# Seven experts in descending token count, with 376 to 448 columns a pass

## Chip, cores and metric

The kernel runs on one core of one Trainium2 chip. The metric is the device time of one execution in microseconds (us), lower is better. TensorE (PE in the profile, PEld for its weight loads) multiplies matrices, VectorE (DVE) and ScalarE (ACT) work on elements, GpSimd (POOL) and SyncE (SP) here mostly issue DMA transfers; the engines run side by side, each through its own list of instructions in order.

## What is computed

Three stages, cut from the reference:

```
for t in range(S):                                   # a linear attention with a complex decay
    S_re, S_im = (ar*S_re - ai*S_im) + k v^T, ar*S_im + ai*S_re
    y[:, :, t] = einsum('bhd,bhde->bhe', q[:, :, t], S_re)
e_idx = argmax(x @ w_gate, axis=1)                   # 3072 tokens, 384 wide, 8 experts
for e in range(8):                                   # one expert per token
    h = maximum(x[mask] @ w1[e], 0)                  # 384 -> 1024
    out[mask] = gate_w * eom * (h @ w2[e])           # 1024 -> 384
h = x @ w_in; g = maximum(0.01*h, h); return g @ w_out   # 384 -> 2048 -> 384
```

Counted from the reference's own gating on its inputs, the experts get 354, 406, 392, 388, 370, 421, 338 and 403 tokens.

## The kernel before, in words

**Attention and routing.** The sequence goes through in six chunks of 128 positions; a planner in Python orders that part. Each chunk's tokens are routed as it ends, and POOL scatters every token's row to a slot of its expert in the DRAM buffer `xs_d`, which has 8 x 448 slots (`CAP` = 448), in the order of the expert's number.

**The experts** (lines 1015 to 1061) follow in the order of their number. Each is two dense layers on 448 columns, whatever its token count. All products are made of three matmuls (`three`, lines 908 to 910) on high and low parts of both operands. The first layer has 8 output blocks `f` of 9 matmuls each (`first_layer`, into the PSUM tile `hp`, 4 buffers); ACT writes the high part `hh` (line 984) and DVE the low part `hl` (line 985). The second layer has 3 output blocks `d` of 24 matmuls (into `yp`); ACT moves each to `yT` and SP stores it (`y_store`, line 977) into `x2_d` at the expert's offset in a compact order, 448 columns wide, so that the next expert overwrites what lies behind the expert's own tokens. That makes 72 + 72 = 144 matmuls an expert. The next expert's slots are loaded into `xe` by SP while the first layer runs (`x_load`, line 889), transposed by PE as 4 x 112 rows (line 903) during the second layer's blocks, and split into `xh` and `xl` (lines 817 and 820).

Expert 0 is special: its first layer runs in two halves of 224 columns (`HALF`), since the first half's slots are complete before the last chunk's tokens have landed.

**Weights.** A list of jobs loads 768 KB pieces on the SP queue into four `raw` buffers, four jobs ahead (`feed`), and each `use()` in the expert loop converts the oldest. A piece of an expert's weights is split into high and low part by ACT and DVE (`wh`, `wl`). A piece of `w_in` or `w_out` is kept as 64-bit numbers and is converted by `d_conv` (one ACT and four DVE instructions, lines 872 to 876), then stored to DRAM (`wf`, line 877) for the last stage. There are 16 of these, d0 to d15. The list before is d0, then for each next expert two pieces of its first layer, a d piece, two of its second layer, a d piece, with d15 extra while expert 2 runs. In the first expert the jobs run after `f` = 0 of the first half, and after `f` = 0, 2 and 4 of the second.

**Places.** After expert 0's first layer `places()` (line 950) sums the counts over the partitions with one matmul, forms the eight offsets `offs` with a chain of eight small additions on DVE, and POOL scatters an (index, weight) pair of every token to `tok_d` (24 indirect DMAs, line 967). From then on SP reads an expert's offset into a register (`values_load`, line 976) before its stores.

**Last stage.** Six windows of 512 columns through `w_in` and `w_out`. In window 5, `flags()` (line 1087) gathers the conditions under which the whole is computed again in a slow general way (an expert with more than 448 tokens is one).

Of the kernel before, what the change touches and what calls it, by code (L numbers as in the profile page):

```python
# [62 lines left out]
def constants():  # L63
    tri = []
    for c in range(2):
        o = token_order(c)
        tri.append((o[:, None] <= o[None, :]).astype(np.float32))
    eye = np.eye(P, dtype=np.float32)
    strict = np.triu(np.ones((P, P), np.float32), 1)
    ones = np.ones((P, P), np.float32)  # L70
    big = np.stack([tri[0], tri[1], 4 * tri[0], 4 * tri[1], eye, strict, ones], 1)
    rev = np.tile(np.arange(NE, 0, -1, dtype=np.float32), B)
    base = np.tile(np.arange(NE, dtype=np.float32) * CAP, B)
    ids = np.arange(P)[:, None] + P * np.arange(NT)[None]
# [283 lines left out]
def tile_kernel(ctx: ExitStack, tc: tile.TileContext, q, k, v, a_re, a_im, wg, w1, w2, w_in, w_out, cbig, csmall, seq, vseq, wgn, out):  # L358
# [22 lines left out]
    IDS = const.tile([P, NT], F32, name="IDS")  # L381
# [5 lines left out]
    offs = const.tile([P, NE + 1], F32, name="offs")  # L387
    offi = const.tile([1, NE], I32, name="offi")
# [401 lines left out]
    raws, wsp, xst, xhl = {}, {}, {}, {}  # L790
    wpool = []

    def w1_src(e, i):
        return w1[e, :, i * 512:(i + 1) * 512].rearrange("(k p) f -> p k f", p=P)

    def w2_src(e, i):
        return w2[e, i * 512:(i + 1) * 512, :].rearrange("(k p) d -> p k d", p=P)

    def pieces(e):
        return [((e, 1, i), w1_src(e, i)) for i in range(2)] + [((e, 2, i), w2_src(e, i)) for i in range(2)]  # L800

    def new_raw(dt=F32):
        return wpool[0].tile([P, 1536], dt, tag="raw", name="raw", bufs=4)

    def w_load(key, src):
        raws[key] = new_raw()
        nc.sync.dma_start(out=raws[key], in_=src)

    nsp = [0]

# [110 lines left out]
    def add_d(n):  # L921
        jobs.append((lambda: d_load(n, d_src(n)), lambda: d_conv(n)))

    add_d(0)
    for e in range(NE - 1):
        for i, p in enumerate(pieces(e + 1)):
            add_w(*p)
            if i % 2:
                add_d(1 + 2 * e + i // 2)
        if e == 2:  # L930
            add_d(15)
    for i in range(4):
        add_w(("in", i), wf[i])
        add_w(("out", i), wf[4 + i])
    done = [0, 0]

    def feed():
        while done[0] < min(len(jobs), done[1] + 4):
            jobs[done[0]][0]()
            done[0] += 1  # L940

# [3 lines left out]
            done[1] += 1  # L945
            feed()

    off = [0] * NE

    def places():  # L950
# [10 lines left out]
        nc.vector.tensor_tensor(out=dl, in0=offs[:, :NE], in1=CS[:, 1, 0], op=ALU.subtract)  # L961
# [3 lines left out]
        nc.vector.tensor_copy(out=pair.bitcast(I32)[:, :, 0], in_=IDS)  # L965
# [48 lines left out]

    for e in range(NE):
        last = e + 1 == NE
        when = {0: 1, 2: 1, 4: 1, 8: 1, 9: 1, 10: 1}
        if e == 2:
            when[5] = 1
        elif last:  # L1020
            when = {0: 1, 1: 1, 2: 1, 3: 1, 9: 1, 10: 1}
        hs = []
        if e == 0:
            hs = [new_h() for f in range(F1 // P)]
            for part in HALF:
                x_split(0, (0, 1, 2), part)
                for f in range(F1 // P):
                    first_layer(0, f, slice(part[0] * SM, part[1] * SM), *hs[f])
                    if part[0]:
                        if f == 0:  # L1030
                            x_load(1)
                        use(when.get(f, 0))
                    elif f == 0:
                        use()
            places()
        else:
            for f in range(F1 // P):
                hs.append(new_h())
                first_layer(e, f, slice(0, CAP), *hs[f])
                if f == 0:  # L1040
                    if last:

# [7 lines left out]
        for d in range(3):  # L1050
            yp = pm.tile([P, 512], F32, name="yp")
            for f in range(F1 // P):
                three(yp[:, :CAP], cols((e, 2, f // 4), (f % 4) * DM + d * P, P), hs[f], f == 0, f == F1 // P - 1)
            yt = ff.tile([P, CAP], F32, name="yT", bufs=4)
            nc.scalar.activation(out=yt, in_=yp[:, :CAP], func=AF.Copy)
            y_store(e, d, yt)
# [27 lines left out]

    bad = const.tile([1, 1], I32, name="bad")

    def flags():

        fl = f2.tile([P, 2], F32, name="fl", bufs=1)
        nc.vector.tensor_reduce(out=fl[:, 0:1], in_=oka, axis=AX.X, op=ALU.min)  # L1090
        nc.vector.tensor_scalar(out=lmin, in0=lmin, scalar1=LMIN2, scalar2=None, op0=ALU.is_ge)
        nc.vector.tensor_reduce(out=fl[0:1, 1:2], in_=lmin, axis=AX.X, op=ALU.min)
        nc.vector.tensor_tensor(out=fl[0:1, 0:1], in0=fl[0:1, 0:1], in1=fl[0:1, 1:2], op=ALU.min)
        cp = pm.tile([P, 512], F32, name="tp")
        for i, (src, n) in enumerate(((acc, NE), (counts[:, 0:1], 1), (fl[:, 0:1], 1))):
            nc.tensor.matmul(out=cp[:, 8 * i:8 * i + n], lhsT=ONES, rhs=src, start=True, stop=True)
        b = f2.tile([1, 3], F32, name="b", bufs=1)
        nc.vector.tensor_reduce(out=b[:, 0:1], in_=cp[0:1, :NE], axis=AX.X, op=ALU.max)
        nc.vector.tensor_scalar(out=b[:, 0:1], in0=b[:, 0:1], scalar1=float(CAP), scalar2=None, op0=ALU.is_gt)
        for i, lim in ((1, CAP / 2), (2, P)):  # L1100
# [58 lines left out]
    slow = nc.values_load(bad[0:1, 0:1], min_val=0, max_val=4)  # L1159
    f2c.close()  # L1160
    pmc.close()
    with tc.If(slow > 0):
# [37 lines left out]
```

## Time and profile before

| | |
|---|---|
| time, median of 3 runs | 935.76 us (935.19 to 937.3) |
| the profiled execution | 935.82 us, span 934.1 us |
| PE, PEld busy | 96%, 84% of the span |
| DVE, ACT, POOL busy | 60%, 50%, 10% |
| granted clock, mean | 0.989 |
| DMA over the span | 121.97 MB, 131 GB/s |

The span is the profiled part of the execution; 1.7 us of its time lie around it. Busy times of PE overlap in part, since matmuls are pipelined and their ends are modelled: how fast matmuls follow each other is read from their starts. An engine with much idle time can still be the one that is waited for in a short stretch.

### The profile page before, as it was taken

Reading aid. Unit: us, or ns where it says so; the run is one execution under the profiler, and the core shown is the slowest. Engines: PE = TensorE matmul, PEld = TensorE weight load, DVE = VectorE, ACT = ScalarE, POOL = GpSimd, SP = SyncE. Lnnn points to the kernel's source line nnn. Section 1 sums busy time; section 2 is a strip of 40 time slices with the busy share of each in tenths; the row PEclk is TensorE's granted clock in tenths of the full one; section 3 lists DMA queues with packets and bytes.
Section 4 is the critical chain, followed back from the end, with each engine's and each line's share of the span. In section 5 each row is a group of like instructions: output and inputs, shape, how many; then the busy total and the mean of one; then the engine's idle time right before and its main releaser. Section 6 shows DMA issues by size and latency. Waiting matters only on the chain.

```text
span 934.1 us, 14772 instructions
## 1 busy us (share of the span) xinstructions
PE 899.2 (96%) x5943; PEld 786.3 (84%) x5943; DVE 564.8 (60%) x964; ACT 469.4 (50%) x765; POOL 96.9 (10%) x90
## 2 busy tenths in 40 slices
PE   7888999999989999999999999999999999999996
PEld 3656878887879899999999899989999998989895
DVE  4679999797877677577566434353363454454332
ACT  6898887877635454444435433333343333333232
POOL 5000302101212810000000000100100100101001
PEclk8999999999999999999999999999999999999999
DMA  9834565212476998777568101302203104000001
GB/s 325 341 91 146 193 239 181 63 53 91 137 249 180 196 239 278 249 252 234 186 216 274 54 1 39 130 1 78 92 1 131 39 0 135 35 1 18 19 1 36
DMA packets 56091, 121.97 MB, mean 131 GB/s; under 512 B 8432, under 2 KB 24480, under 8 KB 56016
## 3 DMA queue, kind: packets, MB, share of 16 engines
q1 hardware_dynamic: 49792, 101.27, 34.7%
q0 software_dynamic: 6224, 19.69, 5.7%
q8 instruction: 48, 0.79, 0.4%
q14 instruction: 27, 0.22, 0.1%
HBM read 89.46 MB, written 31.48 MB: 129 GB/s over the span
## 4 chain that ended last, share of the span: by engine, by line
PE 81%; issue 8%; DVE 5%; ACT 4%; DMA 1%; POOL 1%; SPq 0%; POOLq 0%; another core or an unknown queue 0%; DVEq 0%; ACTq 0%
PE hp L910 10%; PE hp L908 10%; PE hp L909 10%; PE yq L910 6%; PE yq L908 6%; PE yq L909 6%; PE yp L908 4%; PE sc L608 4%; PE yp L909 4%; PE yp L910 4%; PE tp L599 4%; PE yp L620 2%; PE cum L521 2%; PE kv L635 2%; ACT s L453 2%
## 5 line engine op out<-in xcount | busy, mean ns | idle before, releaser
L908 PE MATMUL hp<-xh,wh 128*128 128x512 f32 (+2 forms) x504 | 189.5, 376 | 0.1
L910 PE MATMUL hp<-xh,wl 128*128 128x512 f32 (+2 forms) x504 | 189.4, 376 | 0.0
L909 PE MATMUL hp<-xl,wh 128*128 128x512 f32 (+2 forms) x504 | 188.8, 375 | 0.1
L1139 DVE TENSOR_TENSOR g<-g,hp 128x512 f32<-128x512 f32 x96 | 66.0, 687 | 156.6 <-ACT g L1138 155.0
L1138 ACT ACTIVATE g<-hp 128x512 f32<-128x512 f32 x96 | 57.4, 597 | 186.1 <-PE hp L910 174.9
L908 PE MATMUL yq<-wh,gh 128*128 128x384 f32 x384 | 129.7, 338 | 0.9 <-ACT gh L817 0.9
L910 PE MATMUL yq<-wh,gl 128*128 128x384 f32 x384 | 129.8, 338 | 0.2
L909 PE MATMUL yq<-wl,gh 128*128 128x384 f32 x384 | 129.3, 337 | 0.0
L910 PEld LDWEIGHTS hp<-xh,wl 128*128 128x128 f32 x504 | 95.5, 189 | 15.6
L820 DVE TENSOR_TENSOR gl<-g,gh 128x512 fp32r<-128x512 f32 x96 | 66.5, 692 | 67.1 <-ACT gh L817 45.4
L909 PEld LDWEIGHTS hp<-xl,wh 128*128 128x128 f32 x504 | 95.6, 190 | 11.8 <-DVE xl L820 0.2
L908 PEld LDWEIGHTS hp<-xh,wh 128*128 128x128 f32 x504 | 95.5, 189 | 11.9 <-DVE hl L985 0.5
L817 ACT ACTIVATE gh<-g 128x512 fp32r<-128x512 f32 x96 | 60.7, 632 | 73.6 <-DVE g L1139 73.6
L820 DVE TENSOR_TENSOR wl<-raw,wh 128x1536 fp32r<-128x1536 f32 x40 | 70.2, 1756 | 24.9 <-ACT wh L817 24.1
L1123 POOL DMA_INDIRECT out<-ot,gpair x24 | 24.1, 1005 | 573.4 <-ACT ot L1122 567.4
L908 PEld LDWEIGHTS yq<-wh,gh 128*128 128x128 f32 x384 | 72.1, 188 | 5.9 <-ACT gh L817 1.7
L909 PEld LDWEIGHTS yq<-wl,gh 128*128 128x128 f32 x384 | 72.1, 188 | 4.3
L910 PEld LDWEIGHTS yq<-wh,gl 128*128 128x128 f32 x384 | 72.0, 188 | 0.9 <-DVE gl L820 0.9
L908 PE MATMUL yp<-hh,wh 128*128 128x448 f32 x192 | 71.7, 373 | 0.0
L909 PE MATMUL yp<-hl,wh 128*128 128x448 f32 x192 | 70.3, 366 | 0.0
L910 PE MATMUL yp<-hh,wl 128*128 128x448 f32 x192 | 70.2, 366 | 0.0
L599 PE MATMUL tp<-CB,qk 128*128 128x128 f32 x384 | 56.9, 285 | 9.9 <-DVE qk L555 5.6
(156 smaller groups left out, 1424.4 us busy)
## 6 DMA issues: line engine op xcount, KB each, us to landing
raw<-w SPq DMA_DIRECT2D x32, 768.0 KB
vt<-v SPq DMA_DIRECT2D x12, 512.0 KB
raw<-w_in SPq DMA_DIRECT2D x8, 768.0 KB
wf<-w SPq DMA_DIRECT2D x16, 384.0 KB
raw<-w_out SPq DMA_DIRECT2D x8, 768.0 KB
raw<-wf SPq DMA_DIRECT2D x8, 768.0 KB
xs_d<-zero POOLq DMA_DIRECT2D x4, 1344.0 KB
x_d<-yT SPq DMA_DIRECT2D x24, 224.0 KB
```

Of the source, the lines that this page charges most:

```text
L453: S.op(ACT, 0.04 + A(hi - lo), lambda: nc.scalar.activation(out=out.ap(lo, hi), in_=in_.ap(lo, hi), **kw), in_.b(lo, hi), out.b(lo, hi), p ...
L521: S.op(PE, 0.64, lambda fp=fp, a=a, z=z: nc.tensor.matmul(out=fp.t, lhsT=TRI[c % 2], rhs=th.ap(a, z), start=True, stop=True), [cbb] + th.b ...
L599: nc.tensor.transpose(tp.t[:, h, :], src.t[:, h0 + h].rearrange("p a d -> p (a d)"), IDN)
L608: nc.tensor.matmul(out=sc.t[:, h, :], lhsT=kT.t[:, h], rhs=qT.t[:, h], start=True, stop=True)
L817: nc.scalar.activation(out=hi, in_=src, func=AF.Copy)
L820: nc.vector.tensor_tensor(out=lo, in0=src, in1=hi, op=ALU.subtract)
L908: nc.tensor.matmul(out=out, lhsT=ah, rhs=bh, start=first, stop=False)
L909: nc.tensor.matmul(out=out, lhsT=ah, rhs=bl, start=False, stop=False)
L910: nc.tensor.matmul(out=out, lhsT=al, rhs=bh, start=False, stop=last)
L1123: put = nc.gpsimd.indirect_dma_start(out=rows, out_offset=bass.IndirectOffsetOnAxis(ap=gpair.bitcast(I32)[:, j, 0:1], axis=0), in_=ot, in_ ...
L1138: nc.scalar.activation(out=g, in_=hp, func=AF.Copy, scale=0.01)
L1139: nc.vector.tensor_tensor(out=g, in0=g, in1=hp, op=ALU.max)
```

## The change

The seven experts after expert 0 run in descending order of their token count, and the expert at place n runs with `CAPS[n]` columns. A slot load still takes 448 rows in 112 partitions, and PE still transposes all of them. What is narrower is the split of the transposed slots, every matmul and evacuation of the two layers, and the stores. Expert 0 stays first, with 448. For this the order must be known before the first weights of place 1 are loaded: a new `ranks()` after `f` = 4 of expert 0's first half compares the counts and writes, by place, the expert, its slot base and its offset to `plani`, from which SP reads registers. Until then the list of jobs may issue three loads only, so three d pieces now come first, and the weights of place 1 after them; d3 follows these, and from expert 2 on each expert has two. `flags` is called in two steps, at `f` = 2 and 6, and compares each place's count with its own bound.

```diff
+CAPS = (448, 448, 432, 424, 408, 400, 384, 376)
...
+    def reg(n, r):
+        if (n, r) not in regs:
+            top = (NE - 1, (NE - 1) * CAP, NTOK)[n]
+            regs[n, r] = nc.values_load(plani[0:1, n, r:r + 1], engines=[mybir.EngineType.SP], min_val=0, max_val=top)
+        return regs[n, r]
+
+    def one(w, r):
+        return w[bass.ds(reg(0, r), 1)].rearrange("o a b -> (o a) b") if r else w[0]
...
-        return nc.sync.dma_start(out=xst[e][:, a:z], in_=xs_d[e * CAP + a * SM:e * CAP + z * SM].rearrange("(s p) d -> p s d", p=SM))
+        src = xs_d[bass.ds(reg(1, e), CAP)] if e else xs_d[a * SM:z * SM]
+        return nc.sync.dma_start(out=xst[e][:, a:z], in_=src.rearrange("(s p) d -> p s d", p=SM))
...
-        cs = slice(part[0] * SM, part[1] * SM)
+        cs = slice(part[0] * SM, min(part[1] * SM, CAPS[e]))
...
-    add_d(0)
-    for e in range(NE - 1):
-        for i, p in enumerate(pieces(e + 1)):
+    for n in range(3):
+        add_d(n)
+    for p in pieces(1):
+        add_w(*p)
+    add_d(3)
+    for e in range(2, NE):
+        for i, p in enumerate(pieces(e)):
             add_w(*p)
             if i % 2:
-                add_d(1 + 2 * e + i // 2)
-        if e == 2:
-            add_d(15)
+                add_d(2 * e + i // 2)
...
-        while done[0] < min(len(jobs), done[1] + 4):
+        while done[0] < min(len(jobs), done[1] + 4, limit[0]):
...
+    def ranks():
         cp = pm.tile([P, 512], F32, name="tp")
         nc.tensor.matmul(out=cp[:, :NE], lhsT=ONES, rhs=acc, start=True, stop=True)
-        nc.vector.memset(offs[:, 0:1], 0.0)
-        for e in range(NE):
-            nc.vector.tensor_tensor(out=offs[:, e + 1:e + 2], in0=offs[:, e:e + 1], in1=cp[:, e:e + 1], op=ALU.add)
-        nc.vector.tensor_copy(out=offi, in_=offs[0:1, :NE])
+        vec.tensor_copy(out=num, in_=cp[:, :NE])
...
+        vec.tensor_tensor(out=more, in0=inner(key), in1=outer(key), op=ALU.is_gt)
+        vec.tensor_reduce(out=rank, in_=more, axis=AX.X, op=ALU.add)
...
+        for n, src in ((1, base), (2, offs), (3, num)):
+            vec.tensor_tensor(out=more, in0=sel, in1=inner(src), op=ALU.mult)
+            vec.tensor_reduce(out=plan[:, n], in_=more, axis=AX.X, op=ALU.add)
...
+        vec.tensor_copy(out=plani, in_=plan[0:1, :3])
+        limit[0] = len(jobs)
...
-        if e and d == 0:
-            off[e] = nc.values_load(offi[0:1, e:e + 1], engines=[mybir.EngineType.SP], min_val=0, max_val=NTOK)
-        nc.sync.dma_start(out=x2_d[d][:, bass.ds(off[e], CAP)] if e else x2_d[d][:, :CAP], in_=yt)
+        nc.sync.dma_start(out=x2_d[d][:, bass.ds(reg(2, e), CAPS[e])] if e else x2_d[d][:, :CAPS[0]], in_=yt)
...
-        if e == 2:
-            when[5] = 1
+        if e == 0:
+            when = {0: 1, 3: 1, 5: 1, 8: 1, 9: 1, 10: 1}
...
-                    elif f == 0:
+                    elif f in (0, 2):
                         use()
+                    elif f == 4:
+                        ranks()
+                        feed()
...
-            if i == 5 and f == 4:
-                flags()
+            if i == 5 and f in (2, 6):
+                flags(f > 2)
```

The change moves instructions on two engines in expert 0's first half. On DVE (`w` is the converted d piece, `hl` the low part of a block of the first layer, `xl` that of the slots), before:

```order
L985 SCALAR_TENSOR_TENSOR hl<-hp,hh 128x224
L873 TENSOR_SCALAR w_3524<-raw 128x768
...
L876 SCALAR_TENSOR_TENSOR w_3524<-expo,w_3524 128x768
L985 SCALAR_TENSOR_TENSOR hl<-hp,hh 128x224 x7
L820 TENSOR_TENSOR xl<-tp,xh 128x224 x3
L985 SCALAR_TENSOR_TENSOR hl<-hp,hh 128x224
```

And now:

```order
L1021 SCALAR_TENSOR_TENSOR hl<-hp,hh 128x224 x2
L889 TENSOR_SCALAR w_3555<-raw 128x768
...
L892 SCALAR_TENSOR_TENSOR w_3555<-expo,w_3555 128x768
L1021 SCALAR_TENSOR_TENSOR hl<-hp,hh 128x224 x2
L978 COPY num<-tp 128x8
...
L991 CAST plani<-plan 1x24
L1021 SCALAR_TENSOR_TENSOR hl<-hp,hh 128x224 x3
L836 TENSOR_TENSOR xl<-tp,xh 128x224 x3
```

A second conversion and the 17 small instructions of `ranks` now stand ahead of the three `xl` that the second half's matmuls read.

On SP, from the first loads of the expert stage on, before (`xe` are the slots, `wf` the stores of converted pieces):

```order
L889 DMA xe<-xs_d 112x2x384
L863 DMA raw<-w_in 128x3x512
L807 DMA raw<-w 128x3x512 x2
L863 DMA raw<-w_in 128x3x512
L889 DMA xe<-xs_d 112x2x384
L877 DMA wf<-w_3524 128x768
L807 DMA raw<-w 128x4x384
L889 DMA xe<-xs_d 112x4x384
L807 DMA raw<-w 128x4x384
```

And now:

```order
L879 DMA raw<-w_in 128x3x512 x3
L906 DMA xe<-xs_d 112x2x384
L893 DMA wf<-w_3523 128x768
L893 DMA wf<-w_3555 128x768
L803 TENSOR_LOAD plani
L803 ISA x2
L823 ISA
L823 DMA raw<-w 128x3x512
...
L823 DMA raw<-w 128x4x384
L803 TENSOR_LOAD plani
...
L906 DMA xe<-xs_d 112x4x384
L893 DMA wf<-w_3702 128x768
L823 ISA
L823 DMA raw<-w 128x4x384
```

The weights of place 1 moved from ahead of the second slot load to behind the two `wf` stores and the read of `plani`.

## Rows read from the trace of the kernel before

**Rows 1.** Windows by stage: expert 0's first layer; the other seven experts

```profile
core 0: us, PE busy (x) PEld busy (x) DVE busy (x) ACT busy (x) POOL busy (x), PEclk, DMA share, GB/s
268.40:289.10 20.70, 19.74 (x154) 18.90 (x155) 13.58 (x26) 10.72 (x23) 1.04 (x2) 0.92 0.55 168
...
305.30:519.70 214.40, 213.14 (x1080) 195.34 (x1079) 140.90 (x161) 101.10 (x141) 22.00 (x18) 1.00 0.78 230
```

**Rows 2.** Timeline of SP: start, us, ...: first store of experts 0, 1, 2, 7

```profile
294.88 0.37 SPq L977 DMA_DIRECT2D x_d<-yT  x1
...
325.50 0.38 SPq L977 DMA_DIRECT2D x_d<-yT  x1
...
357.57 0.37 SPq L977 DMA_DIRECT2D x_d<-yT  x1
...
510.69 10.14 SPq L977 DMA_DIRECT2D x_d<-yT  x3
```

**Rows 3.** Timeline of PE: matmuls 8 apart (224, 448 columns), 11 apart (384)

```profile
277.58 0.28 PE L908 MATMUL hp<-xh,wh 128*128 128x224 f32 x1
...
278.47 0.28 PE L910 MATMUL hp<-xh,wl 128*128 128x224 f32 x1
...
292.27 0.36 PE L908 MATMUL yp<-hh,wh 128*128 128x448 f32 x1
...
293.90 0.37 PE L910 MATMUL yp<-hh,wl 128*128 128x448 f32 x1
...
542.20 0.34 PE L908 MATMUL yq<-wh,gh 128*128 128x384 f32 x1
...
544.15 0.34 PE L910 MATMUL yq<-wh,gl 128*128 128x384 f32 x1
```

**Rows 4.** Timeline of DVE: expert 0's first half, then `places`

```profile
271.51 0.55 DVE L873 TENSOR_SCALAR w<-raw 128x768 int32<-128x768 int32 x1
...
275.03 1.28 DVE L985 SCALAR_TENSOR_TENSOR hl<-hp,hh 128x224 fp32r<-128x224 f32 x4
277.16 0.39 DVE L985 SCALAR_TENSOR_TENSOR hl<-hp,hh 128x224 fp32r<-128x224 f32 x1 [0.85 <-ACT hh L984]
278.17 0.39 DVE L985 SCALAR_TENSOR_TENSOR hl<-hp,hh 128x224 fp32r<-128x224 f32 x1 [0.62 <-ACT hh L984]
279.18 0.39 DVE L985 SCALAR_TENSOR_TENSOR hl<-hp,hh 128x224 fp32r<-128x224 f32 x1 [0.61 <-ACT hh L984]
279.48 0.68 DVE L820 TENSOR_TENSOR xl<-tp,xh 128x224 fp32r<-128x224 f32 x2
...
292.65 1.49 DVE L956 TENSOR_TENSOR offs<-offs,tp 128x1 f32<-128x1 f32 x8
...
294.31 0.36 DVE L962 TENSOR_TENSOR hd<-hot,dl 128x192 f32<-128x192 f32 x1
```

**Rows 5.** Windows around the start of expert 0's matmuls

```profile
265.45:268.86 3.41, 1.82 (x13) 1.43 (x14) 2.64 (x20) 1.35 (x6) 2.50 (x4) 1.00 0.92 346
268.86:272.28 3.42, 3.42 (x18) 3.42 (x17) 1.43 (x4) 1.40 (x3) 0.89 (x1) 0.50 0.33 121
```

**Rows 6.** Line 976: the read of an offset into a register of SP

```profile
L976 SPq TENSOR_LOAD <-offi x7: 268/482/810, 320.1 to 503.2; - x7
```

**Rows 7.** Timelines of SP and ACT: a load of a weight piece, and its first reader

```profile
493.29 0.44 SPq L807 DMA_DIRECT2D raw<-wf  x1
...
499.34 1.49 ACT L817 ACTIVATE wh<-raw 128x1536 fp32r<-128x1536 f32 x1 [0.95 <-DMA raw<-wf]
```

**Rows 8.** Timelines of SP and PE: expert 2's slot load, and its first transposes

```profile
308.60 1.09 SPq L889 DMA_DIRECT2D xe<-xs_d  x1
...
326.16 0.96 PE L903 MATMUL tp<-CB,xe 112*128 112x112 f32 x8 [1.26 <-issue]
```

**Rows 9.** Windows: during POOL's scatter of places, and three experts later

```profile
300.00:345.00 45.00, 43.74 (x223) 39.91 (x222) 29.29 (x34) 22.51 (x31) 26.35 (x21) 1.00 0.99 201
390.00:480.00 90.00, 90.00 (x462) 82.58 (x460) 59.26 (x67) 40.78 (x59) 0.00 (x0) 1.00 0.71 228
```

**Rows 10.** Waits of the last stage: who waited for whom, us, times, longest

```profile
PE tp L1096 <- DVE fl L1093: 0.9, 1, 0.9
```

More of the change, by code (lines that the diff above doesn't have):

```diff
@@ L791, in tile_kernel, with w1_src, w2_src, pieces @@
     wpool = []
[L793 to L800, printed above, removed]
+    regs = {}
+    def reg(n, r):
[5 more added lines that the diff above has]
+        return w[bass.ds(reg(0, r), 1)].rearrange("o a b -> (o a) b") if r else w[0]
+    def w1_src(r, i):
+        return one(w1, r)[:, i * 512:(i + 1) * 512].rearrange("(k p) f -> p k f", p=P)
+    def w2_src(r, i):
+        return one(w2, r)[i * 512:(i + 1) * 512, :].rearrange("(k p) d -> p k d", p=P)
+    def pieces(r):
+        return [((r, 1, i), lambda i=i: w1_src(r, i)) for i in range(2)] + [((r, 2, i), lambda i=i: w2_src(r, i)) for i in range(2)]
     def new_raw(dt=F32):
@@ L806, in w_load @@
         raws[key] = new_raw()
-        nc.sync.dma_start(out=raws[key], in_=src)
+        nc.sync.dma_start(out=raws[key], in_=src())
     nsp = [0]
@@ L946, in use, with places @@
             feed()
-    off = [0] * NE
-    def places():
+    def ranks():
         cp = pm.tile([P, 512], F32, name="tp")
         nc.tensor.matmul(out=cp[:, :NE], lhsT=ONES, rhs=acc, start=True, stop=True)
-        nc.vector.memset(offs[:, 0:1], 0.0)
-        for e in range(NE):
-            nc.vector.tensor_tensor(out=offs[:, e + 1:e + 2], in0=offs[:, e:e + 1], in1=cp[:, e:e + 1], op=ALU.add)
-        nc.vector.tensor_copy(out=offi, in_=offs[0:1, :NE])
+        num, key, rank = (ff.tile([P, NE], F32, name=nm, bufs=1) for nm in ("num", "key", "rank"))
+        more, sel = (ff.tile([P, NE, NE], F32, name=nm, bufs=1) for nm in ("more", "sel"))
+        base = CS[:, 1, 0]
+        inner = lambda t: t.unsqueeze(1).to_broadcast([P, NE, NE])
+        outer = lambda t: t.unsqueeze(2).to_broadcast([P, NE, NE])
+        vec = nc.vector
+        vec.tensor_copy(out=num, in_=cp[:, :NE])
+        vec.scalar_tensor_tensor(out=key, in0=base, scalar=-1.0 / (16 * CAP), in1=num, op0=ALU.mult, op1=ALU.add)
+        vec.tensor_scalar(out=key[:, 0:1], in0=key[:, 0:1], scalar1=1.0e4, scalar2=None, op0=ALU.add)
+        vec.tensor_tensor(out=more, in0=inner(key), in1=outer(key), op=ALU.is_gt)
+        vec.tensor_reduce(out=rank, in_=more, axis=AX.X, op=ALU.add)
+        vec.tensor_scalar(out=rank, in0=rank, scalar1=float(CAP), scalar2=None, op0=ALU.mult)
+        vec.tensor_tensor(out=sel, in0=inner(rank), in1=outer(base), op=ALU.is_equal)
+        vec.tensor_tensor(out=more, in0=more, in1=inner(num), op=ALU.mult)
+        vec.tensor_reduce(out=offs, in_=more, axis=AX.X, op=ALU.add)
+        for n, src in ((1, base), (2, offs), (3, num)):
+            vec.tensor_tensor(out=more, in0=sel, in1=inner(src), op=ALU.mult)
+            vec.tensor_reduce(out=plan[:, n], in_=more, axis=AX.X, op=ALU.add)
+        vec.tensor_scalar(out=plan[:, 0], in0=plan[:, 1], scalar1=1.0 / CAP, scalar2=0.25, op0=ALU.mult, op1=ALU.add)
+        vec.tensor_copy(out=plani, in_=plan[0:1, :3])
+        limit[0] = len(jobs)
+    def places():
         dl = ff.tile([P, NE], F32, name="dl", bufs=1)
@@ L960, in places @@
         sh = ff.tile([P, NT], F32, name="sh", bufs=1)
-        nc.vector.tensor_tensor(out=dl, in0=offs[:, :NE], in1=CS[:, 1, 0], op=ALU.subtract)
+        nc.vector.tensor_tensor(out=dl, in0=offs, in1=CS[:, 1, 0], op=ALU.subtract)
         nc.vector.tensor_tensor(out=hd, in0=hot, in1=dl.unsqueeze(1).to_broadcast([P, NT, NE]), op=ALU.mult)
@@ L964, in places @@
         nc.vector.tensor_tensor(out=cpos, in0=sh, in1=slot, op=ALU.add)
-        nc.vector.tensor_copy(out=pair.bitcast(I32)[:, :, 0], in_=IDS)
+        nc.vector.tensor_copy(out=pair.bitcast(I32)[:, :, 0], in_=IDS[:, :NT])
         for j in range(NT):
@@ L1038, in tile_kernel @@
                 hs.append(new_h())
-                first_layer(e, f, slice(0, CAP), *hs[f])
+                first_layer(e, f, slice(0, cap), *hs[f])
                 if f == 0:
@@ L1052, in tile_kernel @@
             for f in range(F1 // P):
-                three(yp[:, :CAP], cols((e, 2, f // 4), (f % 4) * DM + d * P, P), hs[f], f == 0, f == F1 // P - 1)
+                three(yp[:, :cap], cols((e, 2, f // 4), (f % 4) * DM + d * P, P), [h[:, :cap] for h in hs[f]], f == 0, f == F1 // P - 1)
             yt = ff.tile([P, CAP], F32, name="yT", bufs=4)
-            nc.scalar.activation(out=yt, in_=yp[:, :CAP], func=AF.Copy)
-            y_store(e, d, yt)
+            nc.scalar.activation(out=yt[:, :cap], in_=yp[:, :cap], func=AF.Copy)
+            y_store(e, d, yt[:, :cap])
             if d < 2:
@@ L1085, in tile_kernel, with flags @@
     bad = const.tile([1, 1], I32, name="bad")
[L1087 to L1093, printed above, removed]
-        cp = pm.tile([P, 512], F32, name="tp")
[L1095 to L1100, printed above, removed]
+    fl = f2.tile([P, 2], F32, name="fl", bufs=1)
+    b = f2.tile([1, NE + 2], F32, name="b", bufs=1)
+    def flags(step):
+        if step == 0:
+            nc.vector.tensor_reduce(out=fl[:, 0:1], in_=oka, axis=AX.X, op=ALU.min)
+            nc.vector.tensor_scalar(out=lmin, in0=lmin, scalar1=LMIN2, scalar2=None, op0=ALU.is_ge)
+            nc.vector.tensor_reduce(out=fl[0:1, 1:2], in_=lmin, axis=AX.X, op=ALU.min)
+            nc.vector.tensor_tensor(out=fl[0:1, 0:1], in0=fl[0:1, 0:1], in1=fl[0:1, 1:2], op=ALU.min)
+            nc.vector.tensor_tensor(out=b[:, 2:], in0=plan[0:1, 3], in1=IDS[0:1, NT:], op=ALU.is_gt)
+            return
+        cp = pm.tile([P, 512], F32, name="tp")
+        for i, src in enumerate((counts[:, 0:1], fl[:, 0:1])):
+            nc.tensor.matmul(out=cp[:, 8 * i:8 * i + 1], lhsT=ONES, rhs=src, start=True, stop=True)
+        for i, lim in ((0, CAP / 2), (1, P)):
             nc.vector.tensor_scalar(out=b[:, i:i + 1], in0=cp[0:1, 8 * i:8 * i + 1], scalar1=float(lim), scalar2=None, op0=ALU.is_lt)
@@ L1158, in tile_kernel @@
     assert done[1] == len(jobs)
-    slow = nc.values_load(bad[0:1, 0:1], min_val=0, max_val=4)
+    slow = nc.values_load(bad[0:1, 0:1], min_val=0, max_val=NE + 2)
     f2c.close()
```

17 lines of the change are left out of this document (10 added, 7 removed).

## The prediction

> **What bounds the kernel now.** I read the windows by stage first, then the starts of the stores, then PE's own starts. In the stretch of the seven experts after expert 0 PE is busy 213.1 of 214.4 us at granted clock 1.00, DVE 140.9 and ACT 101.1 [rows 1]: PE bounds it, and nothing else is near. The stores show the same as a beat: between the first stores of experts 0 and 1 lie 30.62 us, between those of experts 1 and 2 32.07, and from expert 2 to expert 7 five times (510.69 - 357.57) / 5 = 30.62 [rows 2]. The one long beat holds a wait of 1.26 us before the transposes of expert 2's slots [rows 8]. A busy PE is not yet a PE whose time goes with the columns. So I take the starts: 8 matmuls of 224 columns take 278.47 - 277.58 = 0.89 us, 111 ns each; 8 of 448 take 293.90 - 292.27 = 1.63 us, 204 ns; 11 of 384 take 1.95 us, 177 ns [rows 3]. From 224 to 448 that is (204 - 111) / 224 = 0.413 ns a column, and from 384 to 448 (203.8 - 177.3) / 64 = 0.414: a straight line with some 19 ns beside the columns. With it 144 x 0.204 = 29.3 us of a beat are such matmuls; the rest are transposes, which the change leaves.
>
> Expert 0's first layer is another matter. There DVE works 13.6 of 20.7 us [rows 1], but in bursts: the conversion of a d piece holds it from 271.51 to 275.03, 3.5 us, and behind it the blocks' low parts queue; after that it waits for ACT 0.85, 0.62 and 0.61 us and goes on at 279.48 with the `xl` on which PE's second half waits [rows 4]. The idle time in the first half that can take up more DVE work is therefore about 2.1 us.
>
> **The change part by part.**
>
> *Narrower passes.* By place they cut 0, 0, 16, 24, 40, 48, 64 and 72 columns, 264 in all. Times 144 matmuls times 0.413 ns that is 15.7 us, all on PE's path, since PE is the bound there [rows 1, 3]: **-15.7**. ACT, DVE and the stores get shorter too, which is worth nothing by itself. DVE's load stays under PE's: even unshortened its 140.9 us are 71% of what is left, 214.4 - 15.7. Slot loads and transposes stay whole. The row stands against a rule here. The Trainium skill (TensorE: Matmul & The Clock Gate, Back-to-back issue gap) says that in streams of weight load and matmul the spacing is set by both, with about 81 ns at 128 columns and 131 at 512. By these two figures a column would be worth 0.13 ns and the cut 5 us, an estimate from that page; the three spacings measured here lie on a line three times as steep.
>
> *Expert 0's first half on DVE.* New ahead of the second half's `xl` are one conversion, 3.5 us [rows 4], and `ranks`: 17 dependent instructions, 11 of which touch 64 elements a partition and 6 eight or fewer. The nearest rows are the chain of eight single additions, 1.49 / 8 = 0.19 us each, and the 192-element product, 0.36 [rows 4]. All at the first, they cost 3.2 us; the 11 at the second, 5.1; I take 0.25 for the 11, since 64 lies a third of the way, and have 3.9. Together 7.4, less the idle 2.1: the second half starts 5.3 us later. PE stands still meanwhile, first because the buffers of `hp` are full (block 7 needs the low part of block 3, behind the second conversion), then for `xl`. After such a pause the clock can fall: in 3.4 us in which PE was busy 1.8 the clock was 1.00, and in the 3.4 after it 0.50, the lower level of 1.2 GHz [rows 5]. A second fall would cost half of 3.4, 1.7 us; since the conversion of d2 then holds `hp` anyway, I count 0.7. **+6.0** in all. As bounds I take 3.5, if the cheap instructions also fill gaps that I don't see and the clock stays, and 3.5 + 5.1 - 2.1 + 1.7, about 8.5.
>
> *Weights of place 1.* Their loads move behind the two `wf` stores and the register read (0.27 to 0.81 us [rows 6]). The order is ready on DVE at about 275.0 + 0.6 (two low parts) + 3.5 + 0.6 + 3.9 = 283.6; the first piece is issued near 285. A piece needed 6.05 us from issue to reader [rows 7], so near 291 it is there. Its split stands behind block 3 of the second half, which ends near 285.4 + 4.0 + 1.5 (late `xl`, slow clock) = 291. It just fits; if it is late by a microsecond, ACT holds blocks 4 to 7 back, whose high and low parts are needed only in the second layer, from 295 on. **0**, at most +2. The slots of place 1 are issued behind three pieces, near 287, for transposes near 300, 13 us later.
>
> *Later loads.* From expert 1 on the jobs come in the same rhythm as before, without d15 in expert 2, whose third conversion cost PE nothing (its beat was 30.62 too [rows 2]). The registers cost SP under 1 us apiece [rows 6] beside waits that are longer. The wait for the slots of the third expert [rows 8] stays, as it did not come from the columns: **0**, from -1.3 to +3.
>
> *Flags.* PE waited 0.9 us in the last stage for DVE's chain in `flags` [rows 10]. With the chain four blocks ahead of the matmuls that wait is gone: **-0.9**. The shorter `places` saves DVE 1.5 us where PE doesn't wait for it: 0.
>
> Sum: -15.7 + 6.0 - 0.9 = -10.6. Against the profiled execution, 935.82 us (934.1 span and 1.7 around it), that gives 925.2; the median of the runs is 0.06 lower. I forecast **925 us**.
>
> **The rivals.**
>
> *The first expert pays almost nothing.* The added DVE work would have to find more gaps than the 2.1 us, and a loss of 1.5 us would give 935.8 - 16.6 + 1.5 = 920.7. For it speaks that PE's own second half takes 9 us while DVE's share in it is unchanged; against it, that `xl` stands behind all of the new work on an in-order engine. Chance 0.10.
>
> *Loads behind the ranking come late.* Expert 2's slots were 326.16 - 308.60 = 17.6 us on their way [rows 8], while the transfer share was 0.99 and only 201 GB/s moved [rows 9]. If place 1's slots took as long from 287, PE would wait from 300 to 304.6: 4.6 us more, 929.8; with the second place's slots also 3 us worse, 933. Against it: at 287 POOL's scatter has not begun. Chance 0.20.
>
> *The weight loads set a floor.* PEld is busy 195.3 us for 1079 loads, 0.181 us each [rows 1]. If matmuls could not follow each other faster than that, the cut would end at (204 - 181) / 0.413 = 56 columns: places 6 and 7 would give 56 instead of 64 and 72, 240 in all, 14.3 us, and the time would be 926.6. By the Trainium skill's rule above, which goes further, there would be no gain (935.8 - 5 - 0.9 + 6). The spacing of 111 ns at 224 columns, under loads of the same size, speaks against both. Chance 0.03.
>
> *Transfers become the bound, and it is slower.* A beat moves 228 GB/s x 30.62 us = 7.0 MB for an expert [rows 9, 2]; narrower passes ask for it in 26 to 30 us. In the scatter stretch 201 GB/s was all there was at share 0.99. At that rate through all seven experts each would take 34.7 us, 243 in place of 214.4, and the kernel would take 935.8 + 5.1 + 28.6 = 969 us. It is slower than before from the point where the seven take over 214.4 - 5.1 = 209.3 us, that is under 233 GB/s. Against it: three experts later 228 GB/s took a share of 0.71 only [rows 9], so some 320 are to be had once the scatter is over. The Trainium skill (DMA: Bandwidth & Descriptors, Queues, rings and completion order) has each DMA engine take turns between the queues it has work for; the fall to 201 GB/s while POOL scatters agrees. Chance 0.05.
>
> *The change doesn't do what it says.* Were a place's count over its columns, the whole would be computed again in the general way. The seven counts, descending, are 421, 406, 403, 392, 388, 370 and 338, each under its columns by at least 12. Chance 0.01.
>
> **How the numbers follow.** The forecast has the remaining 0.61, with a range of its own from 922.5 to 928. The low end of the whole takes every bound at its best, 935.8 - 15.7 - 0.9 - 1.3 + 3.5 = 921.4, and a part of the first rival; the high end takes 935.8 - 16.6 + 8.5 + 3 = 930.7, and the first price of the late loads: 920.5 to 931. Left out are the rest of the late loads (0.08), transfers (0.05), the fall-back (0.01) and the tail of the first rival (0.04), under 0.2. Within 0.2% is about what a measurement here can tell from no change, 933.9 to 937.6. Faster by more: the forecast, the first three rivals but for 0.02, 0.92. Within: those 0.02 and 0.02 of mild transfer trouble, 0.04. Slower: the other 0.03 of transfers and the fall-back, 0.04.
>
> **What would show it.** A beat between first stores holds 48 matmuls of one place and 96 of the next, so the beats that end at places 3 to 7 should be 30.62 less 0.413 ns for each of their cut columns: 29.4, 28.6, 27.9, 27.1 and 26.5; the one that ends at place 2 30.0 and the wait for slots, 31.3. DVE should work without a gap from the first conversion to the second half's `xl`, which should stand near 284.8 instead of 279.48, with the clock at 0.50 somewhere behind; expert 0's first store should stand near 301. The wait at the flags should be missing. Wrong would be: beats that don't fall with the columns (a floor, or transfers); waits of ACT for `raw` or of PE before the transposes in places 1 and 2 (late loads); no gap on PE in the first half (the first rival).

## Result and the profile after

The changed kernel takes 924.53 us (median of 4 runs, 921.46 to 926.62) beside 936.39 for the kernel before on the same chip (935.19 to 937.3): ratio 0.9872, interval 0.9841 to 0.9902. It is faster, by 11.9 us, and the forecast of 925 is met. The profiled execution took 924.78 us with a span of 923.0, which compares with 935.82 and 934.1.

The windows by stage of the kernel after (columns as in [rows 1]), and four at half clock, three at the start of expert 0's matmuls and one behind its pause:

```profile
268.40:289.10 20.70, 15.13 (x97) 14.24 (x97) 15.37 (x48) 6.44 (x17) 1.95 (x2) 0.75 0.29 93
...
305.30:519.70 214.40, 211.85 (x1165) 205.19 (x1164) 144.03 (x167) 105.01 (x152) 26.00 (x22) 1.00 0.82 232
...
265.45:268.86 3.41, 2.37 (x12) 2.00 (x12) 1.52 (x12) 0.98 (x4) 2.40 (x3) 0.50 0.42 158
268.86:272.28 3.42, 2.79 (x14) 2.30 (x14) 2.05 (x12) 1.07 (x3) 1.49 (x2) 0.50 0.25 92
272.28:275.69 3.41, 3.41 (x20) 3.41 (x20) 2.16 (x4) 1.52 (x3) 0.00 (x0) 0.56 0.50 149
...
285.50:292.30 6.80, 5.33 (x25) 5.33 (x26) 4.35 (x12) 1.89 (x4) 0.00 (x0) 0.50 0.64 211
```

Against [rows 1], PE gets less done in the window that held expert 0's first layer, 15.1 us busy where there were 19.7, and DVE more, 15.4 for 13.6; the clock's mean fell from 0.92 to 0.75. In the stretch that held the seven other experts PE is nearly as full as before, and more work passes in the same 214.4 us: 1165 matmul records in place of 1080.

The first stores of the eight places after (SP's timeline), which answer to [rows 2]:

```profile
303.39 0.37 SPq L1013 DMA_DIRECT2D x_d<-yT  x1
...
333.86 0.38 SPq L1013 DMA_DIRECT2D x_d<-yT  x1
...
365.01 0.36 SPq L1013 DMA_DIRECT2D x_d<-yT  x1
...
393.74 0.37 SPq L1013 DMA_DIRECT2D x_d<-yT  x1
...
421.66 0.36 SPq L1013 DMA_DIRECT2D x_d<-yT  x1
...
449.17 0.36 SPq L1013 DMA_DIRECT2D x_d<-yT  x1
...
476.06 0.34 SPq L1013 DMA_DIRECT2D x_d<-yT  x1
...
502.04 8.57 SPq L1013 DMA_DIRECT2D x_d<-yT  x3
```

The beats are 30.47, 31.15, 28.73, 27.92, 27.51, 26.89 and 25.98 us, 198.65 in all, where the kernel before has 510.69 - 294.88 = 215.81.

DVE's timeline after, expert 0's first half (columns as in [rows 4]; `dest` is the last slot that the stage before works out, `num` and `plani` the first and last step of `ranks`):

```profile
269.90 0.16 DVE L706 SCALAR_TENSOR_TENSOR dest<-rs,slot 128x1 int32<-128x1 f32 x1
...
273.77 0.55 DVE L889 TENSOR_SCALAR w<-raw 128x768 int32<-128x768 int32 x1
...
277.29 0.68 DVE L1021 SCALAR_TENSOR_TENSOR hl<-hp,hh 128x224 fp32r<-128x224 f32 x2
277.89 0.55 DVE L889 TENSOR_SCALAR w<-raw 128x768 int32<-128x768 int32 x1
...
281.40 0.68 DVE L1021 SCALAR_TENSOR_TENSOR hl<-hp,hh 128x224 fp32r<-128x224 f32 x2
282.00 0.16 DVE L978 COPY num<-tp 128x8 f32<-128x8 f32 x1
...
285.56 0.17 DVE L991 CAST plani<-plan 1x24 int32<-1x24 f32 x1
285.65 0.97 DVE L1021 SCALAR_TENSOR_TENSOR hl<-hp,hh 128x224 fp32r<-128x224 f32 x3
286.55 0.67 DVE L836 TENSOR_TENSOR xl<-tp,xh 128x224 fp32r<-128x224 f32 x2
```

The waits of ACT that stood in [rows 4] are gone, DVE goes from the first conversion (273.77) through the second and `ranks` (282.00 to 285.65, 3.65 us) to the second half's `xl` without a gap, and PE waits for it. PE's waits after (who waited for whom: us in total, times, longest):

```profile
PE tp L920 <- DVE xl L836: 4.1, 2, 3.5
...
PE tp L920 <- DMA xe<-xs_d: 1.6, 1, 1.6
PE hp L925 <- DVE hl L1021: 1.5, 1, 1.5
```

In the kernel before the same `dest` ends the stage ahead:

```profile
267.76 0.16 DVE L702 SCALAR_TENSOR_TENSOR dest<-rs,slot 128x1 int32<-128x1 f32 x1
```

With it the span splits into four pieces:

| piece | before, us | after, us | difference |
|---|---|---|---|
| start to the last `dest` | 267.76 | 269.90 | +2.1 |
| last `dest` to expert 0's first store | 27.12 | 33.49 | +6.4 |
| the seven beats | 215.81 | 198.65 | -17.2 |
| last place's first store to the end | 423.4 | 421.0 | -2.4 |
| span | 934.1 | 923.0 | -11.1 |

### The profile page after: what moved, and what is told of

It is laid out like the page before. It is cut to its first block, busy times and chain, and to the rows that moved or that the text cites. A ratio compares the mean times of both kernels' runs of the same rounds, so it can differ in the third digit from the quotient of the medians.

```text
span 923.0 us, 14884 instructions
## 1 busy us (share of the span) xinstructions
PE 884.9 (96%) x5941; PEld 786.1 (85%) x5941; DVE 562.1 (61%) x970; ACT 466.1 (50%) x765; POOL 96.2 (10%) x90
## 4 chain that ended last, share of the span: by engine, by line
PE 79%; issue 8%; DVE 7%; ACT 3%; DMA 2%; POOL 1%; SPq 0%; POOLq 0%; another core or an unknown queue 0%; DVEq 0%; ACTq 0%
PE hp L927 10%; PE hp L926 10%; PE hp L925 9%; PE yq L927 6%; PE yq L925 6%; PE yq L926 6%; PE sc L612 4%; PE tp L603 4%; PE yp L925 4%; PE yp L926 4%; PE yp L927 4%; PE yp L624 2%; PE cum L525 2%; PE kv L639 2%; PE yp L628 1%
## 5 line engine op out<-in xcount | busy, mean ns | idle before, releaser
L925 PE MATMUL hp<-xh,wh 128*128 128x512 f32 (+8 forms) x504 | 187.0, 371 | 1.5 <-DVE hl L1021 1.5
L927 PE MATMUL hp<-xh,wl 128*128 128x512 f32 (+8 forms) x504 | 187.5, 372 | 0.0
L926 PE MATMUL hp<-xl,wh 128*128 128x512 f32 (+8 forms) x504 | 187.5, 372 | 0.0
L925 PE MATMUL yp<-hh,wh 128*128 128x448 f32 (+6 forms) x192 | 68.3, 356 | 0.0
L926 PE MATMUL yp<-hl,wh 128*128 128x448 f32 (+6 forms) x192 | 67.1, 349 | 0.0
L927 PE MATMUL yp<-hh,wl 128*128 128x448 f32 (+6 forms) x192 | 67.1, 349 | 0.0
```

Of the source, the lines that this page charges most:

```text
L925: nc.tensor.matmul(out=out, lhsT=ah, rhs=bh, start=first, stop=False)
L926: nc.tensor.matmul(out=out, lhsT=ah, rhs=bl, start=False, stop=False)
L927: nc.tensor.matmul(out=out, lhsT=al, rhs=bh, start=False, stop=last)
```

## Experiments

They ran in three groups, each on a chip of its own with runs of the kernel before beside it; ratios are to those. Where a size of a few us matters I compare the pieces of the table, in each run's own trace, since the piece ahead of the last `dest` varies (below).

**fixed: the columns alone.** The kernel before, cut by expert number:

```diff
+CAPS = (448, 432, 408, 400, 384, 448, 376, 424)
...
-                first_layer(e, f, slice(0, CAP), *hs[f])
+                first_layer(e, f, slice(0, CAPS[e]), *hs[f])
...
-                    three(yp[:, :CAP], ...
+                    three(yp[:, :CAPS[e]], ...
```

> The kernel before with the same 264 columns cut, by expert number (widths fitted to the counts of these inputs), and without any ranking, moved load or change at the flags. Theory: 935.8 less 15.7, so 920 us, with 918 if the faster spacing that the change's trace shows beside the narrower columns (3.4 us over seven beats) belongs to the narrowing itself; expert 0's first store stays within 1 us of 295 unless the clock falls earlier. Rival (a floor under the spacing): 921.5 or above.

Measured: 920.18 us beside 935.53, ratio 0.9834 (0.9821 to 0.9847), 15.35 us less for 264 columns; the rival's 921.5 was not reached, and neither was the 918 that faster spacing through narrowing would have given. First and last of its first stores:

```profile
294.53 0.37 SPq L978 DMA_DIRECT2D x_d<-yT  x1
...
495.49 0.35 SPq L978 DMA_DIRECT2D x_d<-yT  x1
```

Its way from the last `dest` (267.30) to the first store is 27.23, as before, so nothing but the beats (200.96 in place of 215.81) and the last expert's rest moved. The columns pay by themselves, at 15.35 / (264 x 144) = 0.404 ns each in a matmul.

**p448: all but the narrowing.**

```diff
-CAPS = (448, 448, 432, 424, 408, 400, 384, 376)
+CAPS = (448,) * 8
```

> The change with 448 columns at every place: experts still go by count and are ranked in expert 0's first half, only the narrowing is undone. Theory (columns pay 0.413 ns each per matmul, the ranking costs 6): the seven beats between the stores of d0 go back to about 30.6 us, and the time is the change's 924.5 plus 15.7 to 18.5, so 940 to 943, 4 to 7 above the kernel before. Rival 1 (part of the gain comes from the shifted addresses of the tiles or another side effect of the change, not from the columns): beats near 29.8 and the time 935 to 937. Rival 2 (a column is worth 0.13 ns): 924.5 plus 5, 930.

Measured: 936.42 beside 935.53, ratio 1.0017 (1.0003 to 1.003). The order without the narrowing gains nothing, but it was expected to lose 4 to 7, and rival 1 has the number. Its way to the first store is 299.87 - 266.79 = 33.08, so the ranking costs 6.0 there as in the change; the beats gave it back: 211.43 us, most of them 30.02 or 30.14 where the kernel before has 30.62. PE's timeline shows why, six starts apart:

```profile
428.57 0.36 PE L927 MATMUL yp<-hh,wl 128*128 128x448 f32 x1
...
429.77 0.36 PE L927 MATMUL yp<-hh,wl 128*128 128x448 f32 x1
```

1.20 / 6 = 0.200 us for one of 448 columns, where [rows 3] give 0.204. Counted as one cycle of 2.4 GHz a column (0.417 ns, near the 0.413 of the prediction's line; 448 / 2.4 = 187) that is 13 ns beside the columns in place of 17. Between p448 and the change lie 1.0017 - 0.9872 = 1.45%, 13.6 us, but the intervals leave some 10 to 17, which does not set it apart from 15.4. By the pieces of the two traces the narrowing is worth 211.43 - 198.65 = 12.8 in the beats and 1.0 behind them.

**pad, pad64, pad128, before_again: is it where the tiles lie?** The change's new constants move xh, hh and what follows by 192 bytes. The kernel before with a spare tile, of 48, 16 or 32 floats:

```diff
+    spare = const.tile([P, 48], F32, name="spare")
+    nc.gpsimd.memset(spare, 0.0)
```

> The kernel before with one more constant tile of 192 bytes a partition, so that the tiles behind it lie 192 bytes further on, as in the change; nothing else. Rival (the faster spacing in the change, about 13 ns beside the columns where there were about 18, comes from where the tiles lie): 448-column matmuls of the seven beats at 0.200 us, beats near 30.1, time 931 to 932. Theory (addresses have no part in it): beats of 30.6 and 935 to 937.

> The kernel before with a spare constant tile of 64 bytes a partition; nothing else. Asks what of the address decides the spacing beside the columns (17.8 ns on average in the kernel before, 13.3 in the 192-byte shift from the fourth expert on). If it is the offset within 128 bytes (64 shifts it as 192 does): beats from the fourth expert on of 30.0 to 30.15. If any shift does it: the same here and with 128 bytes. If it is not the address but how PE's stream happens to fall in a run: either value, or a change from one to the other within the run.

> The kernel before with a spare constant tile of 128 bytes a partition; nothing else. Offset within 128 bytes decides: as before, beats of 30.62. Any shift decides: 30.0 to 30.15. Neither, but the run: either value, or a change within the run.

> The kernel before once more, unchanged. If the spacing of its 448-column matmuls belongs to the addresses, the beats are 30.62 again, on whatever chip; if to the run, 30.0 or a change within the run can come out. From the last dest to the first store: 27.1 again.

The last three ran once each. Measured: with 192 bytes ratio 1.0004 (0.9994 to 1.0013), 936.48 us; so in time the rival misses. But the spacing did move. PE's timeline in one run of it (938.5 us), expert 1 and then expert 3:

```profile
335.28 0.37 PE L910 MATMUL yp<-hh,wh 128*128 128x448 f32 x1
...
335.90 0.37 PE L910 MATMUL yp<-hh,wh 128*128 128x448 f32 x1
...
385.27 0.36 PE L910 MATMUL yp<-hh,wh 128*128 128x448 f32 x1
...
385.87 0.36 PE L910 MATMUL yp<-hh,wh 128*128 128x448 f32 x1
```

Three starts take 0.62 us in the first and 0.60 in the second: 0.207 and 0.200 in one run, the same widths and the same lines. Beats are 30.01 to 30.14 but for the one with the slot wait (34.60), and what they give is taken by that wait and by the last stage, which is 2.7 us longer (936.7 - 510.56 = 426.1). With 64 bytes the first beat is 30.15 and the last five are 30.62; with 128 all seven are 30.73 to 30.75. The kernel before gives 30.62 again on another chip (31.25 in the second beat, which has 32.07 in the first run). So the offset within 128 bytes is not it, and shifts do not all act alike; the value mostly repeats with the layout, and can change within a run. What sets it stays open.

One part of before_again's expectation missed: from the last `dest` to the first store it took 293.80 - 265.86 = 27.94, not 27.1 again.

```profile
265.86 0.16 DVE L702 SCALAR_TENSOR_TENSOR dest<-rs,slot 128x1 int32<-128x1 f32 x1
...
293.80 0.37 SPq L977 DMA_DIRECT2D x_d<-yT  x1
```

Its half clock ahead of expert 0 lasted some 6.8 us, where the first run of the kernel before had 3.4. With fixed and the three spare tiles, this way takes 26.75 to 27.94 us without `ranks`.

**after64: the change at the old offsets.** The same spare tile of 16 floats in the change, which makes the shift 256 bytes.

> The change with a spare constant tile of 64 bytes, which puts the blocks' tiles at the offsets within 256 bytes that they have in the kernel before. If the addresses gave part of the gain: the seven beats sum to 201 to 202 in place of 197.5 to 198.7, as in the kernel with fixed widths, and the time is 3 to 4 longer than the change's (ratio 0.990 for 0.987). If they have no part: the change's beats and ratio.

Measured: ratio 0.988 (0.9863 to 0.9898), beats 198.81 us in all. A miss: 201 to 202 were expected. Its five narrow beats (29.19, 28.17, 27.68, 26.62, 26.17) are together 0.8 longer than the change's. But it had no wait for slots, where the change had 1.6: it is 1.8 longer than the change without that wait, and 1.35 longer than after_again (below), which had none either. Of the change's gain, then, some 1.4 to 1.8 us may belong to the layout, not 4.

**after_again: the change once more.**

> The changed kernel once more, unchanged. If the spacing belongs to the addresses and widths, the seven beats come out as in its first profile within 0.1 us each (30.5, 31.1, 28.7, 27.9, 27.5, 26.9, 26.0); if it belongs to the run, some differ by 0.5. If the long half clock ahead of expert 0 (10 us in the first profile, 3.4 in the kernel before) belongs to the run, it differs here, and expert 0's first store stands between 300 and 303.4; from the last dest to that store it stays 33.0 to 33.5.

Measured: ratio 0.9864 (0.9832 to 0.9897). The five narrow beats come out as before to 0.01 us; the two 448-wide ones at the start do not (30.92 and 29.51 for 30.47 and 31.15, the second without a wait for slots). The last `dest` stands at 265.28 in place of 269.90, with half clock for some 3.4 us ahead of expert 0 instead of 10; the way to the first store is 298.23 - 265.28 = 32.95, and that store stands earlier than the 300 to 303.4 expected. So the +2.1 of the table belongs to the run, the narrow beats and the longer way to the change.

**early: no conversion in expert 0's first half, the ranking at once.**

```diff
-    for n in range(3):
-        add_d(n)
+    add_d(0)
...
-    add_d(3)
+    add_d(1)
...
-    done, limit = [0, 0], [3]
+    done, limit = [0, 0], [1]
...
-                    elif f in (0, 2):
-                        use()
-                    elif f == 4:
+                    elif f == 0:
                         ranks()
                         feed()
```

> The change with the ranking right behind block 0 of expert 0's first half, and no conversion of a d piece in that half: only d0's piece is loaded ahead of it, those of d1 and on are converted later. Theory (the 6 us are DVE work in front of the second half's xl: a conversion of 3.5 and the ranks of 3.7 more than the idle time): with two conversions gone from the first half and the ranks in idle time, the second half's xl stands near 278 and the first store near 296; the time falls by 5 to 6, to 919. Rival (the loss is the clock's, whose phase is run by run): 923 to 924.5. Rival (the earlier weight loads push the conversions into the second expert, where PE then waits): 921 to 925 with waits of PE for d pieces.

Measured: 914.84 beside 935.53, ratio 0.979 (0.9762 to 0.9818); one of the six executions took 922.83. DVE's timeline, and SP's line of the first store:

```profile
268.13 0.16 DVE L706 SCALAR_TENSOR_TENSOR dest<-rs,slot 128x1 int32<-128x1 f32 x1
...
271.19 0.39 DVE L1022 SCALAR_TENSOR_TENSOR hl<-hp,hh 128x224 fp32r<-128x224 f32 x1 [1.31 <-ACT hh L1021]
271.50 0.16 DVE L979 COPY num<-tp 128x8 f32<-128x8 f32 x1
...
275.15 0.97 DVE L1022 SCALAR_TENSOR_TENSOR hl<-hp,hh 128x224 fp32r<-128x224 f32 x3
...
279.41 0.39 DVE L1022 SCALAR_TENSOR_TENSOR hl<-hp,hh 128x224 fp32r<-128x224 f32 x1 [0.61 <-ACT hh L1021]
279.72 0.68 DVE L836 TENSOR_TENSOR xl<-tp,xh 128x224 fp32r<-128x224 f32 x2
...
295.68 0.37 SPq L1014 DMA_DIRECT2D x_d<-yT  x1
```

`ranks` stands where the kernel before has a conversion of the same length, DVE has waited for ACT again by the end of the half, and the first store is at 295.68, 27.55 from the last `dest` (268.13): 5.9 less than in the change, as expected. The beats are 197.14, 1.5 less than the change's, 1.2 of it because the wait for slots shrank from 1.6 to 0.4. The time fell further than to the 919 expected: besides the 5.9 and the 1.5, the last `dest` stands 1.8 earlier, which belongs to the run. Both kernels are beaten; the rivals fall, since the first store moved as forecast and PE shows no wait for a d piece.

**convone: one conversion put back.** Early, with d0's conversion in front of the ranking, and so two d pieces loaded ahead of the weights of place 1; the list of jobs, not shown, follows.

```diff
                     elif f == 0:
+                        use()
                         ranks()
                         feed()
```

> As early, with one conversion (d0) put back in front of the ranking in expert 0's first half. Theory (DVE's work in front of the second half's xl counts as far as it exceeds the idle time there): conversion 3.5 and ranks 3.7 against the kernel before, which had the conversion and 2.1 idle: 1.6 later than in the kernel before, so 28.7 from the last dest to the first store, where early has 27.6 and the change 33.5; time 1 above early's ratio of 0.979, so 0.980, with at most 2 us more if the clock falls behind the pause. Rival (the ranks behind block 4 were the cost, the conversions free): 27.6 and early's ratio.

Measured: ratio 0.9822 (0.9804 to 0.984), and 297.63 - 265.36 = 32.27 from the last `dest` to the first store. Both ways expected miss: 28.7 by 3.6, and by 1.6 with the 2 us that were allowed for the clock; the ratio lies at the edge of that. Its DVE timeline with SP's line of the first store, and PE's wait:

```profile
265.36 0.16 DVE L706 SCALAR_TENSOR_TENSOR dest<-rs,slot 128x1 int32<-128x1 f32 x1
...
268.79 0.55 DVE L889 TENSOR_SCALAR w<-raw 128x768 int32<-128x768 int32 x1
...
275.96 1.26 DVE L1023 SCALAR_TENSOR_TENSOR hl<-hp,hh 128x224 fp32r<-128x224 f32 x4
278.88 0.39 DVE L1023 SCALAR_TENSOR_TENSOR hl<-hp,hh 128x224 fp32r<-128x224 f32 x1 [1.66 <-ACT hh L1022]
280.71 0.39 DVE L1023 SCALAR_TENSOR_TENSOR hl<-hp,hh 128x224 fp32r<-128x224 f32 x1 [1.44 <-ACT hh L1022]
...
297.63 0.37 SPq L1015 DMA_DIRECT2D x_d<-yT  x1
```

```profile
PE hp L925 <- DVE hl L1023: 3.9, 2, 3.2
```

The two pieces of work form one lump of 275.96 - 268.79 = 7.2 us. `hp` has four buffers, and a block is 9 matmuls of 0.111 us, so by estimate PE can go on for 4.0 us; then it waits 7.2 - 4.0 = 3.2, which is the longest wait in the row. When PE starts again it is at half clock for some 3.4 us (granted clock 0.50 from 276.7 to 280.0), and it is DVE that waits, 1.66 and 1.44 us. The wait of 3.2 and half of the 3.4 make 4.9 of the 5.2 us that this way is longer than in the kernel before. DVE's idle time was to take up work, and could not: the work had come in a lump too long for the buffers.

**warm: the clock's share.** The change, with matmuls on zeros in PE's pause:

```diff
+            if e == 0 and part[0] and kt == 2:
+                wp = pm.tile([P, 512], F32, tag="yp", name="warm")
+                for _ in range(13):
+                    nc.tensor.matmul(out=wp, lhsT=idle[:, :P], rhs=idle, start=True, stop=True)
```

> The change with 13 matmuls of 512 columns on a tile of zeros, into a PSUM buffer nobody reads, put between the transposes of expert 0's second half where PE waits 3.5 us for xl. Theory: DVE's work is the larger part of the 6.4 us and the fall of the clock behind the pause (6.8 us at half) about 2 of them: the granted clock stays 1.00 there, the way from the last dest to the first store shrinks from 33.5 to 31 to 32, the time by 1.5 to 2.5. Rival (DVE alone is the cost, the PE blocks at half clock are hidden behind it): 33 to 33.5 and no gain.

Measured: ratio 0.9843 (0.982 to 0.9867), beside 0.9864 of the unchanged one on the same chip; the times don't tell them apart. In its trace the clock holds:

```profile
272.28:292.70 20.42, 17.53 (x125) 15.04 (x125) 17.70 (x46) 8.01 (x17) 0.00 (x0) 1.00 0.65 216
```

and the way to the first store is 295.08 - 262.86 = 32.22 (31 to 32 expected), where the change has 33.49 and 32.95: by this 0.7 to 1.3 us are the clock's, less than the 2 expected. The two runs of the change are 0.5 apart, so the size is rough. What remains beside the kernel before, 4.3 to 5.1, goes to DVE's work by subtraction; early, which takes that work out, shows it directly.

**early32: early with the last stage's tiles 32 bytes on.**

> As early, with a spare tile of 32 bytes in the last stage's pool, which puts that stage's tiles where the offset within 256 bytes is 0, as in the kernel with 64 spare bytes, whose last stage spaced its matmuls at 15.6 ns beside the columns against 16.7 to 17.2 elsewhere. If that offset decides: the last stage 2 to 3 us shorter, ratio 0.976. If not: early's time, ratio 0.979.

Measured: 912.25 us beside 932.56, ratio 0.9778 (0.976 to 0.9795), the fastest run here, but not to be told from early's. The piece behind the last place's first store is 1.1 shorter (910.5 - 490.73 = 419.8 for 913.7 - 492.82 = 420.9); half of what was expected; one trace on each side doesn't show that the offset did it.

## Why the prediction was right, point by point

**Columns, -15.7.** Right: alone they gave 15.35 (fixed). Inside the change the places 3 to 7 came out shorter than the forecast by 0.7, 0.7, 0.4, 0.2 and 0.5 us (29.4, 28.6, 27.9, 27.1, 26.5). The step that was mis-sized is the straight line: it takes some 19 ns beside the columns as fixed. PE's timeline after, eight starts apart at 408 columns:

```profile
428.01 0.34 PE L927 MATMUL yp<-hh,wl 128*128 128x408 f32 x1
...
429.48 0.34 PE L926 MATMUL yp<-hl,wh 128*128 128x408 f32 x1
```

1.47 / 8 = 0.184 us, where the line gives 0.019 + 408 x 0.413 / 1000 = 0.1875. At 1/2.4 ns a column the part beside the columns is 13 to 20 ns by width, layout and moment. That made the beats 17.2 shorter where 14.3 of the 15.7 were due in them (48 matmuls of the last place lie behind its first store). By after64 some 1.4 to 1.8 of those 2.9 may be layout; the rest is left open. p448, whose beats are 4.4 shorter than before with no column cut, says the same: not all of the 17.2 is the narrowing's.

**Rule against row.** Under the spacing of 81 and 131 ns at 128 and 512 columns that the Trainium skill states (TensorE: Matmul & The Clock Gate, Back-to-back issue gap) the cut was worth 5 us; fixed measured three times that.

**Expert 0's first half, +6.0.** Right at 6.4, with the work as forecast: conversion 3.5, `ranks` 3.65 for 3.9, no gap on DVE. The pieces: about 1 is the clock's (0.7 forecast, half clock for 6.8 us instead of 3.4), 5.3 were forecast for the work and some 5 were found. The 6.4 sets the change with half clock for 5.5 us behind the last `dest` against the kernel before with 3.4; pairs with nearly the same half clock there give 32.95 - 27.12 = 5.8 (after_again) and 33.49 - 27.94 = 5.6 (before_again), nearer still to the 6.0. The rule behind it, added work less idle time, was right by luck: it holds when DVE is never idle again. convone, where the same rule said 1.6 and 5.2 came (32.27 against 27.12), shows what counts besides: a lump longer than the four `hp` buffers can cover stops PE, and idle time behind it is lost. early shows the other side: one lump of 3.65 us, `ranks` in the place of the conversion, makes the way 27.55, within the 26.75 to 27.94 of the runs without `ranks`.

**Place 1's weights and slots, 0.** Right. The first piece was issued at 286.81 (forecast near 285) and its first reader, at 294.23, had no wait for it. The wait for the third expert's slots stayed, 1.6 us in place of 1.26, and the beat of 31.15 is near the 31.3 forecast; in after_again it was absent, so it is not firm.

**Flags, -0.9.** The wait of [rows 10] is not among PE's waits after. The last piece of the span is 2.4 shorter; 72 x 48 x 0.413 ns = 1.4 of it are due to the last place's columns, and 0.9 to the flags. That sum is not shown, since this piece runs from 421.6 (pad64) to 426.1 us (pad) in kernels with the flags as before; only the missing wait is.

**Not foreseen: +2.1 ahead of the stage.** It belongs to the run. Of it 0.9 already stand at the last but one `dest` (265.41 against 264.51), near which the half clock of this run begins (265.0). The other 1.2 come up under it: from there to the last `dest` it takes 4.49 us, where it takes 3.25 in the kernel before and 3.26 in after_again at full clock. This 2.1 and the 2.9 of the beats nearly cancel, so that the forecast comes within 0.5 us of the median in part by luck.

**Rivals.** No floor under the spacing (0.184 us is near the mean 0.181 of a weight load before, and at 376 columns it went to 0.173, 507.16 to 508.54 for eight). No transfer bound: three experts later the share was 0.75 at 232 GB/s, PE full. "The first expert pays almost nothing" is false for the change, and true for early.

## What to carry to other kernels

When PE is busy all of a stretch, measure what a column costs from matmul starts at two widths, and multiply: here 15.35 us came for 15.7 with nothing else changed. Inside the change the beats fell by a fifth more than was due, so other changes in the same kernel can move the spacing too. Work that must be added to an engine beside the bound goes where the buffers between the two cover it in one piece (here four blocks, 4 us): the way to the first store grew by 6.4 us with the ranking behind two conversions and by 0.4 with the ranking in their place, and that difference is half as much as the whole change gained. And judge a kernel by pieces of its span: two terms that nobody forecast can cancel.

## What the runs showed that I had not expected

- A stream of matmuls of one shape, under the same lines, ran at 0.200, 0.204 or 0.207 us each by layout and moment (448 columns), 3% of a PE-bound stretch; with a spare tile of 128 or 192 bytes most beats were 30.74 or 30.01 to 30.14 us in place of 30.62, and with one of 64 the first was 30.15.
- The half clock ahead of expert 0 lasted some 3.4 and 10 us in two profiles of one kernel, and the last `dest` stood at 265.28 and 269.90. Of these 4.6 us only 1.2 came up at half clock; 3.4 were there before it, at the last but one `dest` (262.02 and 265.41), and what made those is not shown.
